# An attention and two-stage expert kernel: token gathers, weight loads and gates around a change of stages, put in another order

## The chip, the cores and the metric

The kernel runs on one core of a Trainium2 chip. The metric is device time in microseconds (us), the median of three runs. The engines named below are TensorE (PE for its matmuls, PEld for its weight loads), VectorE (DVE), ScalarE (ACT), GpSimd (POOL) and SyncE (SP); each works through its own list of instructions in order. Transfers are issued by SP, ACT or POOL and carried out by 16 DMA engines that all of them share; the profile calls ACT's transfers queue q10, SP's q1 and POOL's q0.

## The reference

Three parts follow each other. First an attention-like recurrence over 4 x 8 heads of 768 steps with head size 40: a running maximum of gates m, a state C = f C + i v k^T, a normaliser n, and y = sigmoid(o) (C q) / max(|n q|, 1). Its output, 3072 tokens of 320 numbers, goes through a dense layer: h = x w_in (320 to 2048), a piecewise function of h (0 below -1, (h+1)^2/4 in between, h above 1), times w_out (2048 to 320). The result goes through a mixture of 8 experts:

```
logits = x @ w_gate;  expert_idx = argmax(logits);  gate_w = softmax(logits)[expert_idx]
for e in range(8):
    mask = expert_idx == e
    out[mask] = gate_w[mask, None] * (np.maximum(x[mask] @ w1[e], 0) @ w2[e])
```

Which tokens an expert gets is known only on the chip, after the dense layer.

## The kernel before

**Stage one** does the attention and the dense layer together. The 3072 tokens are 24 units of 128, three units make one of 8 groups, and each group goes through the dense layer in 16 steps, so there are 128 steps (0 to 127). One step n is: `mm1(n)`, 8 matmuls into a PSUM tile h (two such tiles exist); `act_a(n)`, two ACT instructions and a DVE instruction (line 736) that leave g in `vg` and free h; `act_b(n)`, a cast on ACT (`gh`, line 742) and a subtraction (`gl`, line 744); and three steps later `mm2`, 9 matmuls. Every product of full precision is made of three matmuls with a high and a low part, hence `xh`/`xl`, `wH`/`wL`, `w1h`/`w1l`, `w2h`/`w2l`. Because there are two h tiles, `mm1(n)` waits for line 736 of step n-2.

After each group its rows, with the logits, are stored to `x2_d` in memory, and `route_a`/`route_b` find each token's place in its expert's list; three `scatter`s of POOL (line 838) write the token numbers into the table `id_d`. The last group's tokens are scattered only in stage two.

**Stage two** runs the experts over slots. A slot is 128 or 256 tokens of one expert. Three **top slots** (0, 1 and 2) take the three experts that lead after seven groups; `plan_top` finds them on DVE near the end of stage one. The other slots are laid out by `tables`, some 40 small DVE instructions that run in stage two, after the last scatters. For each slot s:

- `gather_ids(s)` (line 971): POOL fetches token numbers from `id_d` into `ids`; it waits for the scatters;
- `gather(s)` (line 984): POOL fetches those tokens' rows from `x2_d` into `xr`, after a memset of `xr` in slots 1 and 2;
- `load_w1(s)` (lines 900, 901, 903) and `load_w2(s)` (line 909): ACT issues the expert's weights, 1.28 to 1.5 MB and 1.28 MB, into a raw tile `r`;
- `split_w1` (lines 930 to 933) and `split_w2` (lines 918, 919), in four parts each: a cast on ACT and a subtraction on DVE; one-tile slots use the raw w1 and have no `split_w1`;
- `x_prep` (line 996 on): PE transposes `xr`, ACT and DVE copy it out;
- `gates(s)` (lines 1013 to 1020): DVE, one Exp on ACT (line 1016) and DVE again;
- `up` and `down`: the matmuls; the last `down` scales by the gate (line 1074) and POOL scatters the rows to the output (line 1075).

Stage two has steps of its own from 0: slot 0 has `up` steps 0 to 7, slot 1 has 8 to 11, slot 2 has 12 to 15, slot 3 has 16 to 19, slot 4 has 20 to 27. `down` of a step comes 3.9 steps after it.

**What sets the order.** Nothing is scheduled by the compiler: each piece is put down at a step number, the pieces are sorted by it and written out. A piece has a default step in the code; the table `AT` at the head of the file overrides it by name. So `"l1": {0: 117.03}` says that the load of w1 for slot 0 is written just after step 117. An engine's instructions stand in the order that results, and an instruction that waits holds up all that stands behind it on its engine. Names: `g0` are the top slots' gathers, `l1`, `l2` the weight loads, `sw1` the parts of `split_w1(0)`, `gi`, `ga`, `gt` gathers of numbers, gathers of rows and gates of the later slots, `gate0` to `gate2` the gates of the top slots, `tab` the pieces of `tables`, `xp0` to `xp2` the `x_prep`s of the top slots.

Of the kernel before, what the change touches and what calls it, by code (L numbers as in the profile page):

```python
# [68 lines left out]
    "heads": {0: -15.34, 1: -10.89, 2: -8.06, 3: -2.95, 4: 4.98, 5: 8.32, 6: 14.18, 7: 18.03},  # L69
# [7 lines left out]
    "lasta": {0: 2.89},  # L77
    "lastb": {0: 3.06},
    "lateg": {0: -13.65},
# [67 lines left out]
    "state": {0: -9.46, 1: -7.37, 2: -3.35, 3: 3.45, 4: 8.12, 5: 12.51, 6: 19.21, 7: 23.49, 8: 28.02, 9: 33.82, 10:  # L147
# [3 lines left out]
    "swap": {0: 115.78},  # L151
    "tab": {0: 3.67, 1: 3.76, 2: 5.51, 3: 4.37, 4: 4.97, 5: 4.54, 6: 5.3, 7: 5.74, 8: 4.29, 9: 4.09, 10: 3.96, 11:
# [59 lines left out]
def mlstm_moe_kernel(ctx: ExitStack, tc: tile.TileContext, q, k, v, i_gate, f_gate, o_gate,  # L212
# [5 lines left out]
    NT, DM = out.shape  # L218
# [8 lines left out]
    GT = GU * P  # L227
# [17 lines left out]
    N_TOP, N_PAIR, N_SING, N_OPT, N_RARE = 3, 10, 9, 4, 3  # L245
# [52 lines left out]
    with tc.manual_schedule():  # L298
# [571 lines left out]
        order = [("top", i) for i in range(N_TOP)]  # L870
# [5 lines left out]
        two = [kind == "pair" or s == 0 for s, (kind, _) in enumerate(order)]  # L876
# [95 lines left out]
                out=ids_of[s], out_offset=None, in_=id_d[:, :], in_offset=bass.IndirectOffsetOnAxis(ap=row, axis=0),  # L972
                bounds_check=(E + 1) * RS - 1, oob_is_err=False).ins)

        def gather(s):
            top = order[s][0] == "top"
            p2 = pools["a"] if top else pools["b"]
            m = 2 if two[s] else 1
            rows = NT - GT if top else NT + 1
            xr[s] = x = p2.tile([P, m, XR], F32, tag="xr%d" % m, bufs=(N_TOP - 1 if s else 1) if top else 2, name="xr")  # L980
            if top and s:
                G.memset(x, 0.0)
            for j in range(m):
                G.indirect_dma_start(  # L984
                    out=x[:, j, :], out_offset=None, in_=x2_d[0:rows, :],
                    in_offset=bass.IndirectOffsetOnAxis(ap=ids_of[s][:, j:j + 1], axis=0),
                    bounds_check=rows - 1, oob_is_err=False)
# [219 lines left out]
        def second(last_a, last_b):  # L1207
            LAG = 3
            steps = []
            first = {}  # L1210
            for s in range(NSLOT - N_OPT):
                first[s] = len(steps)
                steps += [(s, i) for i in range(KF2 if two[s] else KF2 // 2)]
            for s in range(NSLOT - N_OPT, NSLOT):
                first[s] = len(steps) - 1
            ev2 = []

            def at_step2(name, t, f):
                ev2.append((place(name, t), len(ev2), f))

            def open_b():
                last_b()
                p2_cm = tc.tile_pool(name="pb", bufs=2, reuse_waits="tile")
                pools["b"] = p2_cm.__enter__()
                pools["bcm"] = p2_cm

            N = len(steps)
            for n, (s, i) in enumerate(steps):
                at_step2(("up", n), n, lambda s=s, i=i: up(s, i))
                at_step2(("down", n), n + LAG + .9, lambda s=s, i=i: down(s, i))  # L1230
            at_step2(("lasta", 0), 2.1, last_a)
            at_step2(("lastb", 0), 3.1, open_b)
            for p in range(4):
                at_step2(("s2", 0, p), 3.15 + 1.2 * p, lambda p=p: split_w2(0, p))
            tgen = tables()
            for y in range(20):
                at_step2(("tab", y), 3.3 + y / 4, lambda: next(tgen, None))
            for s in range(1, NSLOT - N_RARE):
                n0, n1 = first[s - 1], first[s]
                if s >= N_TOP:  # L1240
                    t0, t1 = first[s - 2] + .1, first[s - 2] + 1.1
                    if s == N_TOP:
                        t0, t1 = 8.1, 12.7
                    if s == N_TOP + 1:
                        t1 = 14.1
                    if s >= NSLOT - N_OPT:
                        t1 = first[s - 3] + 2.1
                    at_step2(("gi", s), t0, lambda s=s: gather_ids(s))
                    at_step2(("ga", s), t0 + .1, lambda s=s: gather(s))
                else:  # L1250
                    t1 = (0, 3.1, 8.3)[s]
                if s > 1:
                    at_step2(("l1", s), t1 + .2, lambda s=s: load_w1(s))
                at_step2(("l2", s), t1 + (2.3 if s > 1 else .3), lambda s=s: load_w2(s))
                if s >= NSLOT - N_OPT:
                    continue
                if s >= N_TOP:
                    for j in range(2 if two[s] else 1):
                        at_step2(("xp", s, j), n1 - 2.9 + j, lambda s=s, j=j: x_prep(s, j))
                    at_step2(("gt", s), n1 - .8, lambda s=s: gates(s))  # L1260
                for p in range(4):
                    if two[s]:
                        at_step2(("s1", s, p), n0 - .8 + 1.5 * (s == N_TOP + 1) + p * (n1 - n0 + 1) // 4,
                                 lambda s=s, p=p: split_w1(s, p))
                    t0 = LAG + (2 * p if two[s] else 3 * p // 2 if n1 - n0 > 4 else p) if s > 1 else 8 + p / 2
                    at_step2(("s2", s, p), n0 + t0 + .3, lambda s=s, p=p: split_w2(s, p))
            for t, _, f in sorted(ev2, key=lambda e: e[:2]):
                f()


            for group in OPT:
                s = group[0]
                used = nc.values_load(tabs["es"][0:1, col(s):col(s) + 1], min_val=0, max_val=E)
                with tc.If(used < E):
                    for s in group:
                        if s >= NSLOT - N_RARE:
                            load_w1(s)
                            load_w2(s)
                            gather_ids(s)
                            gather(s)  # L1280
                        x_prep(s, 0)
                        gates(s)
                        for p in range(4):
                            split_w2(s, p)
                        for i in range(KF2 // 2):
                            up(s, i)
                        for i in range(KF2 // 2):
                            down(s, i)
            pools["bcm"].__exit__(None, None, None)
            pools["cm"].__exit__(None, None, None)  # L1290
# [4 lines left out]
        def at_step(name, t, f):  # L1295
            ev.append((place(name, t), len(ev), f))
# [35 lines left out]
        for g in range(NG - 1):  # L1332
            n1 = KF * g + KF - 1 + LAG1
# [50 lines left out]
        at_step(("l1", 0), n1 + 2.6, lambda: load_w1(0))  # L1384
        at_step(("l2", 0), n1 + 4, lambda: load_w2(0))
        at_step(("l1", 1), n1 + 6, lambda: load_w1(1))
        at_step(("g0", 0), n1 + .3, lambda: (gather_ids(0), gather(0), gather_ids(1), gather(1), gather_ids(2), gather(2), tconst()))
        for p in range(4):
            at_step(("sw1", p), n1 + 6 + .7 * p, lambda p=p: split_w1(0, p))
        for j in range(2):  # L1390
            at_step(("xp0", j), n1 + 6.5 + j, lambda j=j: x_prep(0, j))
        at_step(("gate0", 0), n1 + 8, lambda: gates(0))
        at_step(("xp1", 0), n1 + 8.5, lambda: x_prep(1, 0))
        at_step(("gate1", 0), n1 + 9, lambda: gates(1))
        at_step(("xp2", 0), n1 + 9.5, lambda: x_prep(2, 0))
        at_step(("gate2", 0), n1 + 10, lambda: gates(2))
        for t, _, f in sorted(ev, key=lambda e: e[:2]):
            if t < NTOT:
                f()
# [49 lines left out]
```

## Time and profile before

| what | value |
|---|---|
| median of three runs | 842.43 us (837.88 to 843.95) |
| the profiled execution: time | 842.51 us |
| its span, from the first to the last instruction | 840.8 us |
| PE busy in the span | 776.6 us (92%) |
| DVE, ACT, POOL busy | 586.3, 455.1, 279.8 us |
| moved by DMA | 112.02 MB, a mean of 133 GB/s |
| mean granted clock of TensorE | 0.96 of full speed |

The profile is of one execution; its times count from the span's start. Stage one ends and stage two begins near 565 us. The views used below are: the waits of an engine (who waited for whom, us in total, times, longest), windows (what each engine was busy in a stretch), the timeline (single instructions, with the idle time before them and what ended it in brackets), and the DMA queues (packets that ended in a stretch). The releaser in brackets is inferred; where it had long been done, another one, often a DMA, ended the wait.

### The profile page before, as it was taken

What the parts mean: (1) busy time and instruction counts of PE and PEld (TensorE: products, weight loads), DVE (VectorE), ACT (ScalarE), POOL (GpSimd) and SP (SyncE); (2) the same over time, 40 slices, a digit from 0 to 9 for tenths busy, and PEclk for the clock granted to TensorE, in tenths of its full rate; (3) what the DMA queues carried; (4) which work ended last, traced back from release to release, by engine and by line L of the source; (5) the groups of instructions that cost most, each with busy time, mean ns of one, the idle gap of its engine ahead of it and who ended that gap; (6) DMA issues with size and microseconds to landing.
All of it is one profiled execution on the core that took longest, in us unless ns stands there. A gap on an engine that the chain in (4) does not pass through costs nothing. (4 is left out here: it accounts for less than half of the span.)

```text
span 840.8 us, 14744 instructions
## 1 busy us (share of the span) xinstructions
PE 776.6 (92%) x5351; PEld 754.7 (90%) x5351; DVE 586.3 (70%) x1279; ACT 455.1 (54%) x982; POOL 279.8 (33%) x309
## 2 busy tenths in 40 slices
PE   6789998999999999999999999869878999999992
PEld 4669988999999999999999999868868999999992
DVE  6898897677866866757857855547455778787650
ACT  5446454445555555655655545643344667666540
POOL 3776755332322322312312411031241234422310
PEclk8889899999999999999999999989989999999996
DMA  8784573252341353243243001814799888887850
GB/s 174 183 222 130 133 178 70 69 87 62 79 103 45 78 105 66 56 97 66 61 100 82 23 1 31 192 47 97 209 299 289 251 245 252 249 249 232 244 166 9
DMA packets 176336, 112.02 MB, mean 133 GB/s; under 512 B 105616, under 2 KB 165074, under 8 KB 176260
## 3 DMA queue, kind: packets, MB, share of 16 engines
q1 hardware_dynamic: 143988, 47.95, 25.1%
q10 hardware_dynamic: 27472, 52.89, 21.7%
q0 software_dynamic: 4800, 10.19, 4.3%
q8 instruction: 44, 0.72, 0.4%
q14 instruction: 32, 0.26, 0.1%
HBM read 101.94 MB, written 9.88 MB: 133 GB/s over the span
## 5 line engine op out<-in xcount | busy, mean ns | idle before, releaser
L728 PE MATMUL h_ps<-xh,wH 128*128 128x384 f32 x384 | 135.4, 353 | 12.3 <-DVE vg L736 12.3
L761 PE MATMUL y_ps<-wH,gh 128*128 128x328 f32 x384 | 124.4, 324 | 0.2 <-ACT gh L742 0.2
L734 ACT ACTIVATE vg<-h_ps,half 128x384 f32<-128x384 f32 x128 | 74.7, 583 | 89.7 <-PE h_ps L728 77.5
L763 PE MATMUL y_ps<-wH,gl 128*128 128x328 f32 x384 | 120.7, 314 | 0.5 <-POOL gl L744 0.5
L762 PE MATMUL y_ps<-wL,gh 128*128 128x328 f32 x384 | 120.4, 314 | 0.0
L669 POOL TENSOR_TENSOR o_in<-o_in,d 128x320 f32<-128x320 f32 x23 | 27.4, 1193 | 244.2 <-DVE d L666 115.5
L736 DVE SCALAR_TENSOR_TENSOR vg<-vg,h_ps 128x384 f32<-128x384 f32 x128 | 70.2, 549 | 50.2 <-ACT vg L735 48.8
L742 ACT CAST gh<-vg 128x384 fp32r<-128x384 f32 x128 | 65.9, 516 | 64.4 <-DVE vg L736 58.5
L728 PE MATMUL h_ps<-xl,wH 128*128 128x384 f32 x384 | 89.3, 341 | 0.0
L744 DVE TENSOR_TENSOR gl<-vg,gh 128x384 fp32r<-128x384 f32 x118 | 73.2, 621 | 21.3 <-ACT gh L742 20.5
L728 PE MATMUL h_ps<-xh,wL 128*128 128x384 f32 x256 | 87.3, 341 | 0.0
L728 PEld LDWEIGHTS h_ps<-xh,wH 128*128 128x128 f32 x384 | 73.3, 191 | 14.4 <-DVE vg L736 12.5
L1068 PE MATMUL y_ps<-w2h,hh 128*128 128x320 f32 x232 | 76.5, 330 | 2.4 <-ACT w2h L918 1.9
L1052 ACT ACTIVATE hh<-h_ps 128x256 fp32r<-128x256 f32 x116 | 44.2, 383 | 59.2 <-PE h_ps L1043 23.5
L1054 DVE SCALAR_TENSOR_TENSOR hl<-h_ps,hh 128x256 fp32r<-128x256 f32 x116 | 48.3, 421 | 39.4 <-ACT hh L1052 37.5
L919 DVE TENSOR_TENSOR w2l<-r,w2h 128x640 fp32r<-128x640 f32 x72 | 58.1, 821 | 24.9 <-ACT w2h L918 23.5
L1069 PE MATMUL y_ps<-w2l,hh 128*128 128x320 f32 x232 | 73.0, 315 | 1.9 <-DVE w2l L919 1.9
L763 PEld LDWEIGHTS y_ps<-wH,gl 128*128 128x128 f32 x384 | 72.6, 189 | 1.1 <-POOL gl L744 1.1
L761 PEld LDWEIGHTS y_ps<-wH,gh 128*128 128x128 f32 x384 | 72.9, 190 | 0.5 <-ACT gh L742 0.5
L762 PEld LDWEIGHTS y_ps<-wL,gh 128*128 128x128 f32 x384 | 73.0, 190 | 0.0
L1070 PE MATMUL y_ps<-w2h,hl 128*128 128x320 f32 x232 | 72.7, 314 | 0.0
L728 PEld LDWEIGHTS h_ps<-xl,wH 128*128 128x128 f32 x384 | 69.4, 190 | 0.7 <-DVE xl L708 0.7
(244 smaller groups left out, 1959.9 us busy)
## 6 DMA issues: line engine op xcount, KB each, us to landing
r<-in_moe_w_dram ACTq DMA_DIRECT2D x19, 1280.0 KB
fzb<-fz_d SPq DMA_DIRECT2D x23, 512.0 KB
r<-in_moe_w_dram ACTq DMA_DIRECT2D x11, 1024.0 KB
r<-in_moe_w_dram ACTq DMA_DIRECT2D x8, 896.0 KB
r<-in_moe_w_dram ACTq DMA_DIRECT2D x22, 256.0 KB
raw<-in_moe_w_out_dram SPq DMA_DIRECT2D x16, 320.0 KB
x_d<-x SPq DMA_DIRECT2D x7, 588.0 KB
raw<-in_moe_w_in_dram SPq DMA_DIRECT2D x16, 256.0 KB
```

The lines of the kernel that those rows point to most:

```text
L728: PE.matmul(h, lhsT=w, rhs=x, start=(m == 0), stop=(m == len(seq) - 1))
L734: A.activation(out=vg, in_=h, func=AF.Relu, bias=half[:, 0:1], scale=0.5)
L736: V.scalar_tensor_tensor(out=vg, in0=vg, scalar=1.0, in1=h, op0=ALU.min, op1=ALU.max)
L742: A.copy(gh, gt)
L744: (pick(("egl", n), V, G) if n < 26 else V).tensor_tensor(gl, gt, gh.bitcast(F32), op=ALU.subtract)
L761: PE.matmul(y, lhsT=gh[:, sl], rhs=wH[:, i, I1:I3], start=(i == 0), stop=False)
L762: PE.matmul(y, lhsT=gh[:, sl], rhs=wL[:, i, I0:I0 + XW], start=False, stop=False)
L763: PE.matmul(y, lhsT=gl[:, sl], rhs=wH[:, i, I1:I3], start=False, stop=(i == KF - 1))
L919: V.tensor_tensor(w2l[s][:, ks, :], r2[:, ks, :], w2h[s][:, ks, :].bitcast(F32), op=ALU.subtract)
L1068: PE.matmul(y, lhsT=hh[:, t, :], rhs=w2h[s][:, k, :], start=st_, stop=False)
L1069: PE.matmul(y, lhsT=hh[:, t, :], rhs=w2l[s][:, k, :], start=False, stop=False)
L1070: PE.matmul(y, lhsT=hl[:, t, :], rhs=w2h[s][:, k, :], start=False, stop=sp_)
```

## The change

Only the order of pieces changes; the instructions and their sizes stay the same, but for the lines that write them (line numbers of the changed kernel differ by a few). PE's list is the same instruction for instruction, and SP's too.

| piece | step before | step now |
|---|---|---|
| `g0`: token numbers and rows of slots 0 to 2 | 118.48, slot by slot | 118.48, both memsets, three number gathers, then four row gathers |
| `l1` 0, `l2` 0, `l1` 1 | 117.03, 119.45, 120.42 | 120.6, 122.2, 124.2 |
| `sw1` parts 0 to 3 | 121, 122.18, 122.14, 125.29 | 123.6, 124.4, 125.2, 126.2 |
| gates of slots 0, 1, 2 | 126.99, 124.41, 127.22 of stage one | 8.4, 9.4, 10.4 of stage two |
| `tab`, 20 pieces | 3.67 to 12.98 | 3.4 to 8.15, evenly |
| `l1` 2, `l2` 2, `l1` 3, `l2` 3 | 7.56, 11.17, 12.27, 15.21 | 5.3, 8.0, 10.2, 12.3 |
| number gathers of slots 3 to 6 | 7.77, 11.16, 13.61, 12.9 | 7.0, 7.1, 7.5, 7.6 |
| row gathers of slots 3, 4 | 7.95, 11.39 | 7.2, 7.3 |

The code, with a line of the table:

```
-    "l1": {0: 117.03, 1: 120.42, 2: 7.56, 3: 12.27, 4: 15.65, ...
+    "l1": {0: 120.6, 1: 124.2, 2: 5.3, 3: 10.2, 4: 15.65, ...
...
+        def rows_of(s):
             top = order[s][0] == "top"
             p2 = pools["a"] if top else pools["b"]
             m = 2 if two[s] else 1
-            rows = NT - GT if top else NT + 1
             xr[s] = x = p2.tile([P, m, XR], F32, tag="xr%d" % m, ...
             if top and s:
                 G.memset(x, 0.0)
+
+        def gather(s):
+            top = order[s][0] == "top"
+            m = 2 if two[s] else 1
+            rows = NT - GT if top else NT + 1
+            if s not in xr:
+                rows_of(s)
+            x = xr[s]
             for j in range(m):
                 G.indirect_dma_start(
...
-                at_step2(("tab", y), 3.3 + y / 4, lambda: next(tgen, None))
+                at_step2(("tab", y), 3.4 + y / 4, lambda: next(tgen, None))
+            for s in range(N_TOP):
+                at_step2(("gt", s), 8.4 + s, lambda s=s: gates(s))
...
-        at_step(("g0", 0), n1 + .3, lambda: (gather_ids(0), gather(0), gather_ids(1), gather(1), gather_ids(2), gather(2), tconst()))
+        def top_rows():
+            for f in (rows_of, gather_ids, gather):
+                for s in range(N_TOP):
+                    f(s)
+            tconst()
+
+        at_step(("g0", 0), n1 + .3, top_rows)
...
-        at_step(("gate0", 0), n1 + 8, lambda: gates(0))
...
-        at_step(("gate1", 0), n1 + 9, lambda: gates(1))
...
-        at_step(("gate2", 0), n1 + 10, lambda: gates(2))
```

**The list of POOL near the end of stage one**, from the last scatters of stage one (`id_d`) on; `ids` are token numbers, `xr` their rows. Before:

```order
L838 DMA id_d<-tid,posi 29952x1 x3
L971 DMA ids<-id_d,row_6058 128x2
L984 DMA xr<-x_d,ids 128x392 x2
L971 DMA ids<-id_d,row_6058 128x1
L982 MEMSET xr 128x392
L984 DMA xr<-x_d,ids 128x392
L971 DMA ids<-id_d,row_6058 128x1
L982 MEMSET xr 128x392
L984 DMA xr<-x_d,ids 128x392
```

Now:

```order
L833 DMA id_d<-tid,posi 29952x1 x3
L976 MEMSET xr 128x392 x2
L966 DMA ids<-id_d,row_6058 128x2
L966 DMA ids<-id_d,row_6058 128x1 x2
L986 DMA xr<-x_d,ids 128x392 x4
```

The memsets stand first, and no row gather stands ahead of a number gather any more.

**The list of ACT in steps 123 to 126 of stage one**; `w1h`, `w1s` are casts of `split_w1(0)`, `ex` the Exp of slot 1's gates. Before:

```order
L735 ACTIVATE vg<-vg 128x384
L1016 ACT_TABLE_LOAD
L1016 ACTIVATE ex<-ex 128x8
L742 CAST gh<-vg 128x384
L734 ACTIVATE vg<-h_ps,half 128x384
L735 ACTIVATE vg<-vg 128x384
L930 CAST w1h<-r_6103 128x2x256
L931 CAST w1s<-r_6103 128x256
```

Now:

```order
L926 CAST w1s<-r_6237 128x256
L737 CAST gh<-vg 128x384
L729 ACTIVATE vg<-h_ps,half 128x384
L730 ACTIVATE vg<-vg 128x384
L925 CAST w1h<-r_6237 128x2x256
L926 CAST w1s<-r_6237 128x256
```

No Exp stands between the steps of stage one any more; three parts of the split do, at 124.4, 125.2 and 126.2, and the first one at 123.6.

**The list of ACT in steps 10 to 12 (before) and 7 to 10 (now) of stage two**; `r_6920` and `r_6837` are w2 of slot 2, `r_6947` and `r_6901` w1 of slot 3. Before:

```order
L1052 ACTIVATE hh<-h_ps 128x256
L1074 ACTIVATE yo<-y_ps,gt 128x320 x2
L1052 ACTIVATE hh<-h_ps 128x256
L909 ISA
L909 DMA r_6920<-in_moe_w_dram 128x8x320
L1052 ACTIVATE hh<-h_ps 128x256
L896 TENSOR_LOAD ew
L896 ISA x2
L900 ISA
L900 DMA r_6947<-in_moe_w_dram 112x2x1024
```

Now:

```order
L904 DMA r_6837<-in_moe_w_dram 128x8x320
L913 CAST w2h<-r_6637 128x640
L1018 ACT_TABLE_LOAD
L1018 ACTIVATE ex<-ex 128x16
L1054 ACTIVATE hh<-h_ps 128x256
L1018 ACTIVATE ex<-ex 128x8
L913 CAST w2h<-r_6637 128x640 x3
L1054 ACTIVATE hh<-h_ps 128x256
L891 TENSOR_LOAD ew
L891 ISA x2
L895 ISA
L895 DMA r_6901<-in_moe_w_dram 112x2x1024
```

Both loads now stand ahead of the output rows of slot 0 (`yo`), and the gates' Exp stands between the casts of slot 1's w2.

## Rows read from the trace of the kernel before

**Rows 1.** Waits of PE, whole run: line, releaser: us, times, longest.

```profile
PE h_ps L728 <- DVE vg L736: 12.3, 6, 6.7
```

**Rows 2.** Timeline of PE: start, length, engine, line; idle before and releaser.

```profile
527.74 0.44 PE L728 MATMUL h_ps<-xh,wH 128*128 128x384 f32 x1 [1.00 <-DVE vg L736]
...
533.35 0.34 PE L728 MATMUL h_ps<-xh,wH 128*128 128x384 f32 x1
...
540.92 0.45 PE L728 MATMUL h_ps<-xh,wH 128*128 128x384 f32 x1 [1.88 <-DVE vg L736]
...
553.48 0.52 PE L996 MATMUL p_x<-ident,xr 128*128 128x128 f32 x3 [0.71 <-DMA xr<-x_d,ids]
...
560.68 0.69 PE L728 MATMUL h_ps<-xh,wH 128*128 128x384 f32 x1 [6.69 <-DVE vg L736]
...
601.72 0.89 PE L996 MATMUL p_x<-ident,xr 128*112 128x128 f32 x3 [3.21 <-DMA xr<-x_d,ids]
...
625.09 0.58 PE L1043 MATMUL h_ps<-xh,w1h 128*128 128x256 f32 x1 [5.81 <-ACT xh L1002]
```

**Rows 3.** Windows: length, busy of PE, PEld, DVE, ACT, POOL, clock, DMA share, GB/s.

```profile
557.00:563.70 6.70, 3.02 (x10) 3.02 (x11) 4.83 (x13) 4.59 (x11) 2.20 (x8) 0.50 0.16 49
...
585.00:595.00 10.00, 10.00 (x82) 10.00 (x81) 8.65 (x26) 5.34 (x11) 1.21 (x1) 1.00 0.68 131
...
601.50:604.70 3.20, 2.98 (x13) 2.98 (x14) 0.85 (x2) 0.48 (x1) 0.40 (x1) 0.50 1.03 337
...
621.90:628.70 6.80, 3.61 (x15) 3.61 (x16) 5.48 (x11) 4.71 (x12) 4.00 (x4) 0.50 1.03 258
...
640.00:780.00 140.00, 139.31 (x1083) 138.84 (x1082) 111.30 (x248) 94.86 (x229) 47.54 (x43) 1.00 0.82 250
```

**Rows 4.** Timeline of ACT, 520 to 550: the loads' issue, first cast, table load.

```profile
523.66 0.44 ACTq L900 DMA_DIRECT2D r<-in_moe_w_dram  x1
...
525.54 0.52 ACT L742 CAST gh<-vg 128x384 fp32r<-128x384 f32 x1 [4.87 <-DVE kk L948]
...
536.51 0.62 ACT L930 CAST w1h<-r 128x512 fp32r<-128x512 f32 x1 [2.90 <-DMA r<-in_moe_w_dram]
...
547.72 1.28 ACT L1016 ACT_TABLE_LOAD   x1
```

**Rows 5.** Timeline of DVE: the gates of slot 1.

```profile
558.00 0.16 DVE L1013 TENSOR_REDUCE mx<-xr 128x1 f32<-128x8 f32 x1 [9.71 <-DMA xr<-x_d,ids]
```

**Rows 6.** Timeline of POOL: last scatter, first numbers, rows of slot 1.

```profile
523.56 0.97 POOL L838 DMA_INDIRECT id_d<-tid,posi  x1 [0.30 <-issue]
...
538.57 1.05 POOL L971 DMA_INDIRECT ids<-id_d,row  x1 [14.04 <-DVE w1l L932]
...
554.88 1.00 POOL L984 DMA_INDIRECT xr<-x_d,ids  x1 [2.00 <-DMA ids<-id_d,row]
```

**Rows 7.** DMA queues, 524 to 532 us: packets, MB, share of 16 engines.

```profile
q10 hardware_dynamic: 54, 0.22, 74.2%
```

**Rows 8.** DMA queues, 534 to 536 us, POOL's queue.

```profile
q0 software_dynamic: 32, 0.00, 1.1%
```

**Rows 9.** DMA queues, 586 to 594 us, ACT's queue.

```profile
q10 hardware_dynamic: 346, 1.30, 85.0%
```

**Rows 10.** DMA queues, 608.2 to 613.6 us, ACT's queue.

```profile
q10 hardware_dynamic: 969, 1.24, 73.2%
```

**Rows 11.** Timeline of ACT in stage two: loads, cast of slot 4.

```profile
585.97 0.34 ACTq L900 DMA_DIRECT2D r<-in_moe_w_dram  x1
...
609.43 0.40 ACTq L900 DMA_DIRECT2D r<-in_moe_w_dram  x1
...
622.37 0.40 ACT L931 CAST w1s<-r 128x256 fp32r<-128x256 f32 x1 [1.61 <-DMA r<-in_moe_w_dram]
```

**Rows 12.** Timeline of POOL in stage two: numbers and rows of slot 3.

```profile
590.38 1.21 POOL L971 DMA_INDIRECT ids<-id_d,row  x1 [10.56 <-DVE hl L1054]
...
595.10 1.02 POOL L984 DMA_INDIRECT xr<-x_d,ids  x1 [3.51 <-DMA ids<-id_d,row]
```

More of the change, by code (lines that the diff above doesn't have):

```diff
@@ L149 @@
         20: 92.02, 21: 97.82, 22: 104.27, 23: 108.02},
[1 row of a table removed]
[1 row of a table added]
     "swap": {0: 115.78},
-    "tab": {0: 3.67, 1: 3.76, 2: 5.51, 3: 4.37, 4: 4.97, 5: 4.54, 6: 5.3, 7: 5.74, 8: 4.29, 9: 4.09, 10: 3.96, 11:
[1 row of a table removed]
     "tk": {0: -16.67, 1: -11.85, 2: -7.57, 3: -1.43, 4: 4.56, 5: 8.69, 6: 12.19, 7: 19.19, 8: 25.39, 9: 30.36, 10:
@@ L973, in gather_ids @@
                 bounds_check=(E + 1) * RS - 1, oob_is_err=False).ins)
-        def gather(s):
+        def rows_of(s):
             top = order[s][0] == "top"
```

18 rows, old and new, of the table AT are left out of this document.

## The prediction

> **What bounds the kernel now.** I first read the busy shares, then PE's waits, then PE's timeline around the places that the change touches, and from each wait followed back to the transfer behind it. PE is the bound nearly everywhere: between 640 and 780 us it works 139.31 of 140 us at clock 1.00 [rows 3]. What can be won is PE's idle time, and the change touches it in the stretch from 525 to 565 us, where stage one ends, and in the first 20 steps of stage two.
>
> The waits of PE name the biggest one: `mm1` behind `vg`, 12.3 us, the longest 6.7 [rows 1]. The timeline places three of these, of 1.00, 1.88 and 6.69 us [rows 2]. The reader should see that none has a cause on PE or DVE: each time ACT was late with a step of the dense layer, because something else stood ahead on its list.
>
> - The 1.00 us at 527.74: ACT stood 4.87 us at the load of w1(0), whose expert number the plan on DVE had not yet given [rows 4].
> - The 1.88 us at 540.92: the first cast of w1(0) waited 2.90 us for that load, issued at 523.66 and usable at 536.51, so 12.85 us later [rows 4].
> - The 6.69 us at 560.68: the Exp of slot 1's gates stood ahead of act steps, and the gates waited on DVE until 558.00 for slot 1's rows [rows 5].
>
> Why were the rows so late? The last scatter was issued at 523.56, 0.1 us before the load, but the first gather of numbers started only at 538.57, 14.04 us idle [rows 6]. POOL's queue finished the scatter's 32 packets between 534 and 536 [rows 8], after ACT's queue had held 74.2% of the engines' time from 524 to 532 for only 54 packets and 0.22 MB [rows 7]. So the slow load stood ahead of the scatter, and everything behind slid: rows of slot 1 were issued at 554.88 and could be used at 558.00 [rows 5, 6], 3.1 us with little beside them (DMA share 0.16 behind it) [rows 3].
>
> In stage two PE idles 3.21 us before slot 3's `x_prep` (rows not there) and 5.81 us before slot 4's first `up` (its w1 not there) [rows 2].
>
> **The sum** is made against the profiled execution, 842.5 us with a span of 840.8; the median of the runs is 842.43, so the two are one number.
>
> **Gathers ahead of the loads, gates after the steps.** With the load of w1(0) written after step 120.6, nothing large stands ahead of the scatter of 523.56. It should land some 3 us later, as the gather at 554.88 did; three number gathers and four row gathers of about 1.0 us each [rows 6] and two landings of some 3 us then end by about 537. `x_prep` of slot 0 no longer waits, which gives back 0.71. The Exps move to stage two, which gives back 6.69. ACT meets the plan's wait no more, which gives 1.00. Behind the long idle stretch PE worked 3.02 us at clock 0.50 (1.2 GHz) [rows 3]; at full clock that is 1.5 us, so 1.5 comes back. Together 6.69 + 0.71 + 1.00 + 1.5 = **9.9 us**. Bounds: 6.7 if the smaller ones reappear elsewhere, 9.9 if all go.
>
> **The later load of w1(0).** What is late next is this load. From 120.6 to its first cast at 123.6 are 3.0 steps; two steps took 533.35 - 527.74 = 5.61 us [rows 2], so the lead is 8.4 us. Queued behind that cast on ACT are the act steps, and PE waits for them two steps later. The nearest rows for the landing are 12.85 us (the same load, [rows 4]) and 8.0 us: w1(2), issued at 585.97 [rows 11], was through by 594, when ACT's queue had moved 1.30 MB [rows 9]. By the first, the cast waits 4.45 us; a wait of 2.90 cost PE 1.88, so PE idles 1.88 + 1.55 = 3.4 us, 1.55 more than before, and I add 1.5 us of half clock, since behind the 3.21 us gap at 601.72 the clock was 0.50 too [rows 3]. By the second nothing waits and the 1.88 goes. I take the first, because it is the same load at the same place, though it no longer shares with the scatter: +1.55 + 1.5 = **+3.1 us** (bounds -1.9 and +3.1, more if the gathers hold it up). The boundary is worth -9.9 + 3.1 = -6.8.
>
> By the Trainium skill, "DMA: Bandwidth & Descriptors", section "Bandwidth", a 1 MB load to 128 partitions moves in 6.15 us; by it the lead would do, and this term would be -1.9. The trace here contradicts it for w1(0), with 12.85 us, and comes near it for w1(2), with 8.0.
>
> **w2(0) and w1(1)** are issued 2.75 and 3.8 steps later, some 8 and 11 us. w2(0) is first cast at step 3.15 of stage two and w1(1) used at step 8, each over 20 us behind the new issue. Nothing, and if that cover is gone one landing's remainder.
>
> **The gates in stage two.** Three Exps and one table load of 1.28 us [rows 4] now stand among the casts of slot 1's w2. From 585 to 595 ACT was busy 5.34 of 10 us [rows 3], which hides them; DVE was busy 8.65 of 10 there, so it is the tighter side. Without the cover some 2 us. The gate numbers are needed by the first output rows, after step 11. I put nothing.
>
> **Numbers and rows of slot 3.** The table piece that gives slot 3's row was the fifteenth in order, at 7.55, and is now at 6.9. From w1(2)'s issue (7.56) at 585.97 to w1(4)'s (15.65) at 609.43 [rows 11] a step took 2.9 us; 0.65 of one is 1.9 us. The numbers, issued at 590.38, were followed by the rows at 595.10 [rows 12], and PE got them at 601.72. I take **-1.9** of the 3.21 us (bounds -3.2, and in the other direction the rival C).
>
> **Weights of slots 2 and 3 earlier.** w1(4) was issued at 609.43 [rows 11], but ACT's queue gave 1.24 MB to w2(3) until 613.6 [rows 10]. With w2(3) issued 2.9 steps earlier, w1(4), for which the second cast still waited at 622.37 [rows 11], can start up to 4.2 us sooner: the 5.81 us of PE's wait would become 1.6, and of the 3.61 us of work at half clock behind it [rows 3] 1.8 would come back, 6.0 together. But the DMA share from 621.9 to 628.7 is 1.03 [rows 3], so part of what is gained returns as the next load's lateness. The ends are 0 and -6.0; I take the middle, **-3.0**.
>
> Sum: 842.5 - 6.8 - 1.9 - 3.0 = 830.8, so **831 us**.
>
> **The rivals.**
>
> A, the load lands fast. Freed of the scatter and the two loads behind it, w1(0) lands in 8.0 us like w1(2): no wait at the first cast, 3.4 + 1.5 us less than forecast, **826 us**. For it speaks w1(2); against it, that only 0.22 MB moved in the first 8 us, when hardly anything else was asked for [rows 7].
>
> B, stage two gains nothing. The DMA engines are full where slot 4's weights load, so the same bytes end at the same time in whatever order, and slot 3 keeps its wait: 842.5 - 6.8 = **836 us**. For it, the shares of 1.03 [rows 3]; against it, a share of 0.68 from 585 to 595, so there is room to load earlier.
>
> C, slower: slot 3's gathers are caught behind an early weight load as the last scatter was, which took some 11 us (523.56 to 534 and later). Numbers to use of rows took 601.72 - 590.38 = 11.3 us; w1(2) now is issued at 5.3, w2(2) at 8.0, on either side of them. If each of the two gathers takes the load's 12.85 us, 25.7 us, and they start 1.9 us earlier, PE waits 12.5 us more: 842.5 - 6.8 + 12.5 = **848 us**. It decides once the two take 20 us together. Against it: the present gathers already stand right behind w1(2), and take 11.3.
>
> **How the numbers follow.** About 1% (8.4 us) is what a measurement can tell from no change. Forecast 0.42, with its own range from 826 to 835; A 0.24; B 0.22; C 0.12. Faster means under 834: nearly all of the forecast (0.40), A (0.24) and a little of B, 0.65. Slower means over 851: the end of C, with a load that also delays slot 4, 0.06. The rest, 0.29, is no change. The range reaches down to A with the full gain of stage two, 842.5 - 9.9 - 1.9 - 1.9 - 6.0 = 823, less 2 for what else falls away, 821; and up past B to 840, into the beginning of C.
>
> **What would show it.** Right, if the last scatter's packets end near 525 and the first number gather starts at about 527; if slot 0's `x_prep` has no wait and no idle time of 6.7 us is left on PE; if PE idles once, some 3 to 4 us, with ACT's first `w1h` cast waiting for its load behind it, and a clock of 0.50 for a few us after; if the wait before slot 3's `x_prep` is under 2 us and that before slot 4's first `up` 2 to 4. A shows as no wait at that cast; B as the same waits of 3.2 and 5.8; C as a wait of over 8 us before slot 3's `x_prep`. The forecast is wrong if the scatter is late though no load stands ahead of it, since then the gathers' lateness has another cause, or if the gates' DVE work holds up the `hl` of the `up` steps.

## The result and the profile after

The changed kernel took **832.64 us** (median of four runs, 829.14 to 836.16), before 843.19; the ratio is 0.9856 with an interval of 0.9821 to 0.9890, some 12 us. Timed again beside later kernels it was 0.9871 (0.9842 to 0.9901). The forecast was 831, 821 to 840, faster. The profiled execution took 834.11 us with a span of 832.4 (before 842.51 and 840.8).

The spans differ by 8.4 us only, since the two executions are not equally long where the change touches nothing. PE's list is the same, so each matmul of before has its partner after: that of 505.05 stands at 508.44, 3.4 us later. In the profiles of this study that matmul starts 0.7 to 7.1 us later than in that of before. So I compare from this matmul on, in stretches between four matmuls (505.05, 585.32, 605.38 and 645.57 in before): A holds the boundary of the stages, B the work in front of slot 3, C slots 3 and 4. All numbers are differences to before in us, one execution each; the ratios are of the timed runs. e6 has no row, since its one profiled execution was 10.9 us longer than the median of its runs.

| kernel | A | B | C | rest | sum | ratio (interval) |
|---|---|---|---|---|---|---|
| the change | -11.05 | +4.73 | -7.64 | +2.17 | -11.8 | 0.9856 (0.9821 to 0.9890) |
| the change again | -12.51 | +5.44 | -8.05 | +2.61 | -12.5 | 0.9871 (0.9842 to 0.9901) |
| e1 boundary alone | -11.04 | -3.98 | +4.78 | +1.16 | -9.1 | 0.9870 (0.9832 to 0.9908) |
| e2 stage two alone | -0.72 | +4.90 | -3.88 | +0.50 | +0.8 | 0.9985 (0.9959 to 1.0010) |
| e3 loads alone | -10.65 | +0.05 | -2.10 | +1.97 | -10.7 | 0.9892 (0.9858 to 0.9926) |
| e4 gates alone | -1.15 | -2.57 | -1.79 | +1.96 | -3.6 | 0.9997 (0.9967 to 1.0027) |
| e5 gather order alone | -3.23 | +0.40 | +0.71 | -0.28 | -2.4 | 0.9949 (0.9917 to 0.9981) |
| e7 no scatters | -11.05 | +0.38 | -8.70 | +4.62 | -14.8 | one run |
| e8 w1(2) earlier | -11.03 | +3.34 | -7.95 | +1.06 | -14.6 | 0.9864 (0.9806 to 0.9922) |
| e9 four loads moved | -10.99 | -4.39 | -0.59 | +2.09 | -13.9 | 0.9850 (0.9822 to 0.9878) |
| e10 e9, memsets later | -12.00 | -3.95 | -0.78 | +4.19 | -12.5 | 0.9809 (0.9781 to 0.9837) |
| e11 gates back | -7.78 | +5.91 | -8.00 | +1.47 | -8.4 | 0.9854 (0.9805 to 0.9903) |

PE's timeline after, the rows that answer to [rows 2]:

```profile
531.71 0.44 PE L723 MATMUL h_ps<-xh,wH 128*128 128x384 f32 x1 [1.59 <-DVE vg L731]
...
598.24 0.89 PE L998 MATMUL p_x<-ident,xr 128*112 128x128 f32 x3 [6.96 <-DMA xr<-x_d,ids]
...
617.18 0.39 PE L1045 MATMUL h_ps<-xh,w1h 128*128 128x256 f32 x1 [1.54 <-ACT xh L1004]
618.82 0.50 PE L1045 MATMUL h_ps<-xl,w1h 128*128 128x256 f32 x2 [0.78 <-DVE xl L1005]
```

The waits of 6.69, 1.88 and 0.71 us are gone; that of 1.00 has become 1.59. In all of A PE's idle time fell from 12.3 to 3.6 us. The wait before slot 3 has grown from 3.21 to 6.96, that before slot 4 fallen from 5.81 to 1.54 and 0.78.

POOL's timeline at the boundary (to be read beside [rows 6]):

```profile
526.95 0.97 POOL L833 DMA_INDIRECT id_d<-tid,posi  x1 [0.31 <-issue]
527.92 0.82 POOL L976 MEMSET xr<- 128x392 f32 x2
535.54 1.07 POOL L966 DMA_INDIRECT ids<-id_d,row  x1 [6.81 <-DVE gl L739]
...
539.63 1.00 POOL L986 DMA_INDIRECT xr<-x_d,ids  x1 [0.30 <-DMA ids<-id_d,row]
...
545.03 1.00 POOL L986 DMA_INDIRECT xr<-x_d,ids  x1 [1.79 <-DMA ids<-id_d,row]
```

From the last scatter's issue to the first number gather it is 8.6 us, not 15.0. The releaser named is not the true one: the gather waits for all three scatters, whose last completion the trace has at 534.72. And ACT, with the load of w1(0) and its first cast:

```profile
538.03 0.44 ACTq L895 DMA_DIRECT2D r<-in_moe_w_dram  x1
...
546.96 0.60 ACT L925 CAST w1h<-r 128x512 fp32r<-128x512 f32 x1
```

The cast has no bracket: nothing was waited for. The load had 8.9 us, and had landed.

### The profile page after: what moved, and what is told of

Read it like the earlier page. It is cut to its first block, busy times and chain, and to the rows that moved or that the text cites. A ratio compares the mean times of both kernels' runs of the same rounds, so it can differ in the third digit from the quotient of the medians.

```text
span 832.4 us, 14739 instructions
## 1 busy us (share of the span) xinstructions
PE 777.6 (93%) x5351; PEld 754.9 (91%) x5351; DVE 587.9 (71%) x1279; ACT 454.6 (55%) x982; POOL 281.9 (34%) x309
```

## The experiments

**e1 and e2, one place each.** e1 keeps the boundary's part of the change and puts the table pieces, gathers and loads of slots 2 to 6 back; e2 is the opposite.

```
e1: "l1" 2: 5.3 -> 7.56, 3: 10.2 -> 12.27; "l2" 2: 8.0 -> 11.17, 3: 12.3 -> 15.21
    "gi" 3 to 6, "ga" 3 and 4, "tab": as before
e2: before, with "l1" and "l2" of slots 2 and 3, "gi", "ga", "tab" of the change
```

> The change at the end of stage one alone (gathers, loads of slots 0 and 1, split, gates); table pieces, loads and gathers of slots 2 to 6 at their steps of before. In the two profiles the work behind the stage boundary is 11.1 us earlier with the change, slot 3's wait is 4.6 us worse and slot 4 gives back 7.5 us. Theory, the two places add: about -11 us against before (831 us), PE's wait for slot 3's rows back near 3.2 us and that for slot 4's weights near 5.8. Rival, stage two is bound by its transfers and takes back what the boundary gains: 836 us or more, with longer waits for weights in slots 2 to 5.

> The change in stage two alone (table pieces, loads, gathers of slots 2 to 6); end of stage one as before, gates of the top slots there too. Theory, the places add: slot 3 +4.6, slot 4 -7.5, later +1.8, so -1 us, within 1% of before. Rival, the early loads help only as the boundary moved with them: slot 4 gains under 3 us and the kernel is 2 to 4 us slower than before.

e1 gave 0.9870 and e2 0.9985: by the timed runs the places add, and the gain is the boundary's. By the traces they don't: the two sums make -8.3 us, the change has -11.8, and its B and C are not those of e1 and e2 added (+0.9 each, against +4.73 and -7.64). By the place the expectation for e1 missed too: its timeline has 0.58 us before slot 3 instead of 3.2, and 7.38 before slot 4, for rows and not for weights:

```profile
593.55 0.54 PE L995 MATMUL p_x<-ident,xr 128*112 128x128 f32 x3 [0.58 <-DMA xr<-x_d,ids]
...
604.06 3.31 PE L1048 MATMUL h_ps<-xs,r 112*128 112x128 f32 x12 [2.63 <-DMA r<-in_moe_w_dram]
...
619.61 0.90 PE L995 MATMUL p_x<-ident,xr 128*128 128x128 f32 x3 [7.38 <-DMA xr<-x_d,ids]
```

**e3, e4, e5: the boundary's parts alone**, each put into the kernel before.

```
e3: "l1" 0: 117.03 -> 120.6, 1: 120.42 -> 124.2; "l2" 0: 119.45 -> 122.2
    "sw1": 121, 122.18, 122.14, 125.29 -> 123.6, 124.4, 125.2, 126.2
e4: -at_step(("gate0", 0), ...), gate1, gate2
    +for s in range(N_TOP): at_step2(("gt", s), 8.4 + s, lambda s=s: gates(s))
e5: -lambda: (gather_ids(0), gather(0), gather_ids(1), ...)   +top_rows
```

> Before, with only the loads of w1 and w2 of slots 0 and 1 and the split at the late steps. Theory, the load of w1(0) stood ahead of the scatter's landing and of the number gathers: the first number gather starts some 8 us after the last scatter's issue instead of 15, the gates of slot 1 some 6 to 8 us earlier, PE's 6.7 us wait shrinks to 0 to 2: 833 to 836 us. Rival, the chain numbers, rows, numbers, rows is slow by itself, since its later half runs under the late load: the wait stays over 4 us and the gain under 3 us.

> Before, with only the gates of slots 0 to 2 moved to steps 8.4, 9.4 and 10.4 of stage two. Theory, PE waited 6.7 us only because an Exp stood ahead of act steps on ACT: that wait goes, the rows of slots 1 and 2 are as late as before, PE waits some 1 to 3 us for them at their x_prep: -5 to -8 us, 835 to 837. Rival, PE needs those rows at the same place in its own list, and waits 5 us or more for them at the x_prep of slots 1 and 2: gain under 3 us.

> Before, with only the order of the top slots' gathers changed (both memsets, three number gathers, four row gathers); the load of w1(0) still ahead of them, gates in stage one. Theory, the late load is what freed the scatter: the first number gather still starts 14 to 15 us after the last scatter's issue, the three numbers land together under the loads some 9 us later, rows of slot 1 then land some 3 to 4 us earlier than before, PE's 6.7 us wait shrinks to 3 or 4: -2 to -4 us. Rival, the order was the fault: the wait goes and the gain is 8 us or more.

The late loads alone give 0.9892 in time, and 10.65 us in stretch A where the change gives 11.05. These two aren't quite alike: the change's A holds 3.4 us at half clock, which cost it 1.5 us, and e3's A none. By PE's idle time in A, 12.3 us before, the loads alone leave 5.4 and the change 3.6. e3's POOL and PE:

```profile
525.80 0.97 POOL L836 DMA_INDIRECT id_d<-tid,posi  x1 [0.31 <-issue]
...
534.56 1.06 POOL L969 DMA_INDIRECT ids<-id_d,row  x1 [7.79 <-DVE vg L734]
```

```profile
558.47 0.51 PE L994 MATMUL p_x<-ident,xr 128*112 128x128 f32 x3 [2.58 <-DMA xr<-x_d,ids]
```

The number gather starts 8.8 us after the last scatter. PE waits for an act step only at the plan (0.76 us), though the gates are still in stage one, and 2.58 us are left, for rows. The gates alone are the rival's case, 0.9997: an act step still waits 2.98 us, and then PE itself waits 4.39 us for the rows. e4's PE:

```profile
548.54 0.69 PE L725 MATMUL h_ps<-xh,wH 128*128 128x384 f32 x1 [2.98 <-DVE vg L733]
...
569.37 0.86 PE L993 MATMUL p_x<-ident,xr 128*112 128x128 f32 x3 [4.39 <-DMA xr<-x_d,ids]
```

The order of the gathers alone, with the load still ahead (e5), starts its first numbers 16.2 us after the last scatter (14 to 15 expected) and gains 3.2 us in A (0.9949), as the theory had it:

```profile
526.81 0.97 POOL L838 DMA_INDIRECT id_d<-tid,posi  x1 [0.30 <-issue]
...
543.03 1.06 POOL L971 DMA_INDIRECT ids<-id_d,row  x1 [14.44 <-DVE w1l L932]
```

**e11, the change without the gates' move**, run last.

```
"gate0" 126.99, "gate1" 124.41, "gate2" 127.22 of stage one; no gates at 8.4, 9.4, 10.4 of stage two
```

> The changed kernel with only the gates of slots 0 to 2 back at their steps of stage one. Theory, with late loads and number gathers first the rows are there before any gate asks for them, so the Exps hold nobody up and their move was not needed: the stretch from the matmul at 505.05 to that at 585.32 is 10 to 11.5 us shorter than before, as with the change (11.05 and 12.51 in two profiles). Rival, the gates still wait for rows, or the table load of 1.28 us and three Exps hold the act steps: the stretch gains under 9 us.

By the number the rival was right: A gains 7.8 us, and PE's idle time there is 7.5 us against 3.6. No gate waits for rows now, but the table load and the Exps stand among the act steps. They are not the whole cause: ahead of the table load ACT's first two casts waited for the load of w1(0), 0.86 and 1.73 us (with the change not at all in the first profile, and 0 and 0.32 us in the second). So the act steps behind were late by the load too:

```profile
544.98 0.62 ACT L925 CAST w1h<-r 128x512 fp32r<-128x512 f32 x1 [0.86 <-DMA r<-in_moe_w_dram]
547.33 0.41 ACT L926 CAST w1s<-r 128x256 fp32r<-128x256 f32 x1 [1.73 <-DMA r<-in_moe_w_dram]
...
551.37 1.28 ACT L1018 ACT_TABLE_LOAD   x1
...
559.63 0.22 ACT L1018 ACTIVATE ex<-ex 128x16 f32<-128x16 f32 x1 [1.49 <-DVE ex L1017]
```

```profile
554.95 0.45 PE L723 MATMUL h_ps<-xh,wH 128*128 128x384 f32 x1 [1.44 <-DVE vg L731]
...
561.92 0.39 PE L1045 MATMUL h_ps<-xh,w1h 128*128 128x256 f32 x1 [1.53 <-DVE vg L731]
```

The 1.53 us stand behind the Exp of 559.63; how the 1.44 us share out between load and table load is open. The new order of the gathers thus brought nothing on top of the late loads as long as the gates stood in stage one: e3, with the old order, has 5.4 us idle in A. The timed runs (0.9854) don't resolve any of this; it is the reading of one trace each.

**e7 and e8: why a load is slow at its start.** w1(2), issued at 574.60 by the change, moved as little in its first 6 us as w1(0) had before. e7 leaves out the last group's three scatters, so that its tokens miss in the experts' lists; e8 puts w1(2) ahead of these scatters.

```
e7: -scatter(NG - 1, j)   +did("scat", NG - 1, j)
e8: "l1" 2: 5.3 -> 3.2
```

> The changed kernel with the three scatters of the last token group left out (their tokens then miss from the experts' lists, the work stays the same). Theory, 4096-byte packets of a weight load take 1 to 2.5 us each while a scatter has not landed, and 0.2 to 0.3 us else: without these scatters w1(2), issued near 575, moves over 0.8 MB in its first 5 us instead of 0.2, and PE's wait before slot 3 falls under 4 us. Rival, the first packets of that load are slow for a reason of their own: they stay at 1 us or more, and so does the wait of 7 us.

> The changed kernel with w1 of slot 2 loaded at step 3.2 of stage two instead of 5.3, ahead of the last scatters and of w2(1). Theory, the load then runs before the scatters' landing, with packets of 0.2 to 0.3 us, and is through in 6 us; from step 8 only w2(2) stands before slot 3's numbers: the wait before slot 3 falls from 7.0 to 3 to 5 us, 2 to 4 us faster than the changed kernel. Rival, w2(1) now meets the scatters instead and is slow in its place, so that slot 1's second half waits: no gain.

The DMA queues in the first 6 us behind w1(2)'s issue (packets, MB, share of the 16 engines), first with the change, then in e7:

```profile
q10 hardware_dynamic: 48, 0.20, 90.6%
```

```profile
q10 hardware_dynamic: 349, 1.31, 78.6%
```

The same load moves 6.5 times as much when no scatter is under way. By the packets' own records a 4096-byte packet took 1.8 us on its engine with the scatters (the median of 48; half of them between 0.7 and 2.3), without them 0.23 (the median of 319). The wait before slot 3 fell to 3.01 us in e7:

```profile
591.98 0.89 PE L998 MATMUL p_x<-ident,xr 128*112 128x128 f32 x3 [3.01 <-DMA xr<-x_d,ids]
```

e8 shows that it is the window and not the load: w1(2) ahead of the scatters is quick, and w2(1), now behind it, is slow. Windows of e8, of the first load and of the second (length, busy of PE, PEld, DVE, ACT and POOL, clock, DMA share, GB/s):

```profile
571.00:576.00 5.00, 4.62 (x23) 4.62 (x24) 3.46 (x17) 0.58 (x2) 3.22 (x3) 0.66 0.95 274
...
580.00:586.00 6.00, 5.93 (x48) 5.70 (x47) 5.50 (x23) 0.77 (x2) 0.00 (x0) 1.00 0.48 30
```

The scatters suffer as well: the last one, issued at 573.85, was complete at 587.08 by its completion records, 13.2 us later, and the number gather followed it by 14.1 us, though DVE had its row at 585.1. The wait before slot 3 was 3.73 us, as the theory had it, and the ratio, 0.9864, is no better than that of the change, as the rival had it:

```profile
599.68 0.89 PE L997 MATMUL p_x<-ident,xr 128*112 128x128 f32 x3 [3.73 <-DMA xr<-x_d,ids]
```

**e6, w2(2) late alone** (`"l2" 2: 8.0 -> 11.17` in the change).

> The changed kernel with w2 of slot 2 loaded at its step of before (11.17 instead of 8.0). Theory, this load stands ahead of slot 3's number and row gathers: numbers land 3 to 4 us after their issue instead of 7.1, PE's wait of 7.0 us before slot 3 falls to 2 to 3, 3 to 5 us faster than the changed kernel unless the load is then late for slot 2. Rival, the slow w1(2) and the early w1(3) hold the gathers: the wait stays over 5 us.

The runs gave 0.9768 (0.9708 to 0.9829, three of them), against the change's 0.9856 (0.9821 to 0.9890) not resolved. Its trace is not compared, so the wait before slot 3 stays open.

**The change again, e9 and e10**, in five rounds side by side.

```
e9:  "l1" 2: 5.3 -> 7.4, 3: 10.2 -> 11.2; "l2" 2: 8.0 -> 10.6, 3: 12.3 -> 12.6
e10: e9, and  -for f in (rows_of, gather_ids, gather):  +for f in (gather_ids, rows_of, gather):
```

> The changed kernel itself, beside the two below. From the matmul at 505.05 on, the first profile showed it 11.8 us ahead of before: a ratio near 0.986, and a wait near 7 us before slot 3.

> The changed kernel with w1(2) loaded at 7.4, w2(2) at 10.6, w1(3) at 11.2, w2(3) at 12.6 (5.3, 8.0, 10.2, 12.3 in it). Theory, a load that meets the scatters while they land is slow and makes them late, and loads ahead of gathers delay these: with w1(2) issued when the scatters have landed and w2(2) behind the row gathers, the numbers land 3 to 4 us after their issue, the rows 3 to 5, and the 7.0 us wait before slot 3 falls to 0 to 2, 4 to 6 us faster than the changed kernel (ratio near 0.98). Rival, stage two is bound by the bytes: what slot 3 gains, PE waits for w2(2), w1(3) or slot 4's weights; the time stays within 2 us of the changed kernel.

> The one before, with the two memsets of xr between the number gathers and the row gathers instead of ahead of both. Theory, POOL's memsets ran beside the plan on DVE and stretched one of its small operations (1.28 us instead of 0.2 to 0.4), so PE's wait near 530 was 1.6 us in every kernel with the memsets first and 0.8 to 1.0 in every other: it falls to about 0.8, the row gathers start at most 0.9 us later, which nobody waits for: 0.8 us faster. Rival, the delay of the row gathers costs as much: no difference.

In e9 the numbers of slot 3 are there 4.6 us after their issue, the wait is gone, and PE waits elsewhere:

```profile
588.40 0.54 PE L996 MATMUL p_x<-ident,xr 128*112 128x128 f32 x3 [0.18 <-DMA xr<-x_d,ids]
...
595.50 0.42 PE L1068 MATMUL y_ps<-w2h,hh 128*128 128x320 f32 x1 [2.12 <-ACT w2h L911]
...
599.26 1.19 PE L1049 MATMUL h_ps<-xs,r 112*128 112x128 f32 x4 [1.90 <-DMA r<-in_moe_w_dram]
```

B is 9.1 us better than with the change, C 7.1 worse: the rival held for most of it, 2 us are left, and the ratio (0.9850) doesn't tell them from nothing. From 590 to 630 e9 keeps the DMA engines at a share of 1.05:

```profile
590.00:630.00 40.00, 33.55 (x225) 32.13 (x224) 21.48 (x50) 18.37 (x43) 10.89 (x10) 0.87 1.05 309
```

In e10 PE's wait at the plan is 0.75 us, as expected. The cause in one row of DVE's timeline each, e9's (memsets on POOL beside it) and e10's:

```profile
524.75 1.27 DVE L948 TENSOR_SCALAR kk<-kk,m 128x8 f32<-128x8 f32 x1
```

```profile
528.16 0.43 DVE L948 TENSOR_SCALAR kk<-kk,m 128x8 f32<-128x8 f32 x1
```

e10 had a median of 830.47 us beside 835.50 of the change and 845.98 of before, 0.9809 against 0.9871, intervals apart, though only just (0.9837 and 0.9842). e6 has a lower ratio, from three runs and with a wider interval. The traces don't show where e10's lead would come from: its sum, -12.5, is that of the change again, and over e9 they show the 0.8 us at the plan and, in sum, no lead; the difference to e9 lies within the intervals.

## Why the prediction was right

The time came out 1.6 us from the forecast, and the boundary and slot 4 were the places of the gain. But the terms were wrong in both directions and cancelled: A was 4.2 us better than the forecast's -6.8, slot 3 6.6 worse than its -1.9, C 4.6 better than the -3.0, and 2.2 were given back behind. That the sum is so near is luck. Of the signs that it had named for being right, no wait before slot 0, no idle time of 6.7 us and some 2 us before slot 4 (1.54 and 0.78) came. A first number gather near 527 (it was 535.54), a `w1h` cast that waits for its load and under 2 us before slot 3 (6.96) did not.

- **The load stood ahead of the scatter: right, and the main thing.** e3 shows it. The size of the landing was wrong. "Some 3 us later" was the price of a row gather; the last scatter took 7.8 us to land with an idle DMA (526.95 to 534.72). Of the 15.0 us of before the load had caused 6.4. What the forecast named as a sign against itself, a late scatter with no load ahead, came half true, and the steps from there to slot 1 had enough room.
- **The later load of w1(0): the step that failed.** It was priced with 12.85 us to land and +3.1 in the sum. It landed within 8.9, rival A's case, and the 1.88 us went as well. The 12.85 were no property of this load but of its place beside the scatters: by the packet records its last packet ended 14.1 to 15.5 us after the issue in the four profiles with the early load (before, e2, e4, e5), and 7.2 to 8.2 us after it in eight with the late one. In e11 it took 10.1, so the lead of 8.4 us that the forecast worked out has little to spare. By the Trainium skill, "DMA: Bandwidth & Descriptors", section "Bandwidth", a 1 MB load issued by GpSimd moves in 6.15 us; the trace after is no slower, with 1.52 MB by ACT's queue between 539 and 545, and where it was far slower, before, a scatter was under way.
- **The 1.00 us at the plan: wrong.** ACT's wait for the expert number was not the cause. DVE has the plan ahead of line 736 of a step in its list; the wait stayed in every kernel, 0.75 to 1.02 us with the memsets later and 1.58 to 1.63 with them first. The plan's second `kk` operation took 1.27 to 1.29 us and ended 0.03 us behind POOL's second memset in every kernel with the memsets first; it took 0.43 us in every other. By the Trainium skill, "SBUF — State Buffer", section "SBUF: two separate sides", VectorE and GpSimd share a pair of ports: of a GpSimd instruction and a VectorE one in a mode that uses the pair, the one that starts first holds it for its whole length, and the other is blocked. The trace after fits that by the ends, 528.77 on DVE and 528.74 on POOL. That DVE's operation was in such a mode, and which of the two held the ports, is not shown: by the records DVE had started 0.43 us ahead of the memsets.

```profile
527.49 1.28 DVE L950 TENSOR_SCALAR kk<-kk,m 128x8 f32<-128x8 f32 x1
```

- **The gates: right in the sum, but not by themselves.** The 6.69 us went with the loads (e3). Alone the gates' move gave 1.15 us in A (e4), on top of the other two 3.3 by the trace (e11), of which a part is the load's there.
- **Half clock: right.** After, one stretch at 0.50 (1.2 GHz) is left in A, from 568.3 to 571.7, behind idle pieces of 0.76 and 1.09 us; before there were two. The change's second profile has none there, with the same idle pieces (0.76 and 1.08), which is the 1.5 us by which its A is better.

```profile
568.30:571.70 3.40, 2.94 (x12) 2.95 (x13) 2.78 (x11) 0.00 (x0) 2.79 (x3) 0.50 0.98 328
```

- **Slot 3: wrong sign.** The numbers were to be earlier by 0.65 of a step. DVE worked through the tables with little idle time in both kernels (1.2 of 14 us before, 2.1 after), and the gather left 0.8 us after DVE had written its row. Against PE nothing moved: it left 590.38 - 583.25 = 7.1 us earlier, in a kernel that was 7.7 us ahead. From the numbers' issue to PE's use of the rows it took 15.0 us instead of 11.3, behind w1(2), which had met the scatters, and w2(2) (e7, e9). This is the mechanism of rival C at a quarter of its size.

The row in before, then row, numbers and rows after:

```profile
589.39 0.23 DVE L1204 TENSOR_SCALAR row<-k,pp 128x9 int32<-128x9 f32 x1
```

```profile
582.26 0.22 DVE L1206 TENSOR_SCALAR row<-k,pp 128x9 int32<-128x9 f32 x1
...
583.25 1.54 POOL L966 DMA_INDIRECT ids<-id_d,row  x1 [11.04 <-DVE hl L1056]
...
590.62 1.00 POOL L986 DMA_INDIRECT xr<-x_d,ids  x1 [4.51 <-DMA ids<-id_d,row]
```

- **Slot 4: right, and under-sized.** The wait of 5.81 went to 2.3, and in all of C PE's idle time fell from 8.5 to 2.5 us and its loss at half clock from 3.3 to 1.7. I had halved the term, since the DMA engines were full; halving was too much. But part of it is time that slot 3 lost, in which the loads ran on: B and C together gained 2.9 us, where the forecast had 4.9. e9 shows that rival B is alive: what slot 3 gains there, slot 4 loses.

## What to carry over

Ask of a late gather which transfer it waits for and what ran beside it: here the costliest wait, on PE, came from a weight load issued 0.1 us behind a scatter, four waits away. Don't take a load's landing time from a place with a scatter under way, and look for the transfer behind the releaser when an engine is named that had long been done. Where the transfers fill the time, a moved load moves the wait: judge it by the sum over the stretches, not by the wait that it cures.

## What the runs showed of the hardware

- Three scatters of 128 four-byte numbers, issued at 524.30, 525.67 and 526.95 in the trace after, took 5.5, 6.9 and 7.8 us from issue to completion with nothing else moving, though their packets were through by 530 and took some 0.01 us each. A load on ACT's queue is slow while scatters land: 0.20 MB in 6 us against 1.31 without them (e7). No run shows why.
- It holds for 1280-byte packets too: w2(1) moved 30 GB/s in e8's window from 580 to 586.
- Two profiles of one kernel differ by 1.5 us in stretch A by a half-clock period alone, and the first 505 us of PE's same list differ by up to 7 us between profiles.
